# Moving an untaken branch ahead of the last copies, and one more drain on GpSimd

## The chip, the cores and the metric

The kernel runs on one core of one Trainium2 chip. The metric is the device time of one execution in microseconds (us); lower is better. The engines are PE (matmuls; PEld is its weight load), DVE (VectorE), ACT (ScalarE), POOL (GpSimd) and SP (SyncE, which here issues loads). Each engine has a sequencer that runs its queue in order; a "q" behind an engine's name marks an instruction that the sequencer itself runs, such as a wait, a branch or a drain.

## The reference

Windowed attention over (8, 8, 576, 64), whose output rows are then routed, one expert a token, through a mixture of eight two-layer networks:

```python
scores = np.where(mask, scale * q @ k.T, -1e9)        # 0 <= i - j < 64
attn = exp(scores - max); attn /= sum(attn) + 1e-9
x = (attn @ v) reordered to (4608, 512)
logits = xn @ en.T / tau                               # rows of x and emb, normalised
expert_idx = argmax(logits, axis=1)
out[mask_e] = gate_w[mask_e, None] * (np.maximum(x[mask_e] @ w1[e], 0) @ w2[e])
```

Here w1 is (8, 512, 1024) and w2 (8, 1024, 512), all float32. How many tokens an expert gets is known only when the kernel runs.

## The kernel before, in words

The first third computes attention tile by tile and puts each finished row of x into a table in DRAM, sorted by expert, with an indirect DMA that POOL issues (`place`, L444, 36 of them). The rest works through the table in groups. A group is one expert's rows: kind F is two slots of 128 rows, kind H one slot. 21 groups (`GS`, numbered 0 to 20; 39 slots) always run; how many rows each expert has decides which expert a group serves. Up to six further groups follow, each inside a branch (`tail`, L997, nested): they run only if the tokens need more groups than the fixed ones. With the inputs timed here the branch is passed over.

`step(g)` (L938) overlaps three groups: it splits group g's second-layer weights into two parts (`renew`, ACT casts L151 and DVE subtracts L154), has SP load the next group's (`load2`, L837), finishes the slots of group g-1, runs the first layer of group g+1 (L861, or L898 for kind H) and then the second layer of group g (L920). `finish(a)` (L925) is ACT's copy of a slot's result out of PSUM, scaled by the gate (L929), into one of four `o` buffers, and then POOL's indirect DMA that scatters the 128 rows to `out` (L930). The order in each engine's queue is the order in which these calls are written.

Group 20 is of kind H. Step 19 finishes the two slots of group 18, step 20 the two of group 19, and after the loop the one slot of group 20 is finished. Then every engine loads the number of groups (`values_load`, L1200) into a register, compares it (L997), jumps over the further groups, and runs a few semaphore instructions in their place. The kernel's closing lines (drains, a handshake of all engines, clearing of semaphores) have the line of the launch, L1220; its opening ones L1212. PSUM has four banks in the ring `ph` (first layer) and four in the ring `po` (second layer).

Of the kernel before, what the change touches and what calls it, by code (L numbers as in the profile page):

```python
# [46 lines left out]
GS = len(ALWAYS)  # L47
NH = ALWAYS.count("H")
KIND = ALWAYS + "F" * ((N + EARLY * P) // 256 + E - 1 - GS)
SLOT = []  # L50
# [35 lines left out]
def attention_moe(ctx, tc, q, k, v, emb, tau, w1, w2, kc, kt, out):  # L86
    nc = tc.nc
# [12 lines left out]
    def weave(*chains):  # L100

        chains = list(chains)
        while chains:
            chains = [c for c in chains if next(c, chains) is not chains]


    rings, turn = {}, {}
# [9 lines left out]
    def take(name):  # L117
        key, tiles = rings[name]
        turn[key] += 1
        return tiles[(turn[key] - 1) % len(tiles)]  # L120
# [598 lines left out]
    xb, xt, xp, ph, hp, po = {}, {}, {}, {}, {}, {}  # L719
# [8 lines left out]
    def load_x(a):  # L728

        src, b = rows(a), take("xb")  # L730
        xb[a] = b
        for q in range(4):
            note(a, nc.sync.dma_start(b[32 * q:32 * q + 32].rearrange("i (t f) -> i t f", t=4),
                                      src[:, q * P:(q + 1) * P].rearrange("(t i) f -> i t f", i=32)))

    def load_rest(*slots):

        for a in slots:
            note(a, nc.sync.dma_start(rest[:, a], rows(a)[:, DM:ROW]))
# [25 lines left out]
    def x_parts(a):  # L765
        x_turned(a)
        x_hi(a)
        x_lo(a)
# [9 lines left out]
    def gate_root(k):  # L778
        a0, a1 = BATCH[k]
        t, m, t0, t1 = gk[k] = [take("gin")[:, :a1 - a0]] + [take("gsm")[:, :a1 - a0] for _ in range(3)]  # L780
        gk[k] += [rest[:, a0:a1, :E], rest[:, a0:a1, C_SS - DM]]
        nc.gpsimd.tensor_tensor(out=t1, in0=gk[k][5], in1=half.to_broadcast([P, a1 - a0]), op=ALU.pow)

    def gate_logits(k):

        t, m, t0, t1, L, ss = gk[k]
        sh = list(t.shape)
        nc.vector.reduce_max(out=m, in_=L, axis=AX.X)
        yield
        nc.vector.tensor_scalar(out=t0, in0=t1, scalar1=1e-30, scalar2=None, op0=ALU.max)  # L790
        yield
        nc.vector.tensor_tensor(out=t, in0=L, in1=m.unsqueeze(2).to_broadcast(sh), op=ALU.subtract)
        yield
        nc.vector.reciprocal(t1, t0)
        yield
        nc.vector.tensor_tensor(out=t1, in0=ss, in1=t1, op=ALU.mult)
        yield
        nc.vector.tensor_tensor(out=t0, in0=t0, in1=t1, op=ALU.add)
        yield
        nc.vector.tensor_scalar(out=t0, in0=t0, scalar1=0.5, scalar2=1e-6, op0=ALU.mult, op1=ALU.add)  # L800
        yield
        nc.vector.reciprocal(t1, t0)
        yield
        nc.vector.tensor_tensor(out=t, in0=t, in1=t1.unsqueeze(2).to_broadcast(sh), op=ALU.mult)
        yield

    def gate_exp(k):
        t = gk[k][0]
        nc.scalar.activation(t, t, AF.Exp)

    def gate_out(k):
        t, m = gk.pop(k)[:2]
        a0, a1 = BATCH[k]
        if k:
            nc.vector.copy_predicated(rest[:, a0:a1, C_TOK - DM].bitcast(I32), again[:, a0:a1].bitcast(U32),
                                      ct[:, NT:].to_broadcast([P, a1 - a0]))
            yield
        nc.vector.reduce_sum(out=m, in_=t, axis=AX.X)
        yield
        nc.vector.tensor_scalar(out=m, in0=m, scalar1=1e-9, scalar2=None, op0=ALU.add)  # L820
        yield
        nc.vector.reciprocal(gate[:, slice(*BATCH[k])], m)
        yield
# [5 lines left out]
    def load1(g):  # L829
        e = expert(g)  # L830
        for c in range(4):
            nc.sync.dma_start(out=w1raw[c], in_=w1v[ds(e, 1), :, c].rearrange("o p f -> (o p) f"))

    def load2(g):
        e = expert(g)
        for c in range(4):
            nc.sync.dma_start(out=w2raw[c], in_=w2v[ds(e, 1), :, c].rearrange("o p k f -> (o p) k f"))  # L837

    def renew(raw, hi, lo):
        for c in range(4):  # L840
            split_hi(c, raw, hi)
        for c in range(4):
            split_lo(c, raw, hi, lo, nc.vector)
# [4 lines left out]
    def parts(g):  # L848

        return 512 // rows_of(g)  # L850
# [32 lines left out]
    def layer1_part(g, part):  # L883
        if KIND[g] == "H":
            return layer1_half(g, part)
        for f in range(parts(g) * part, parts(g) * (part + 1)):
            layer1(g, f)
        hidden(g, part)
# [14 lines left out]
    def turn_half(g, i):  # L903

        ph[g, i] = take("ph")
        for f in range(4):
            nc.tensor.transpose(ph[g, i][:, f * P:(f + 1) * P], hr[g, i][:, f * P:(f + 1) * P], ident)
        hidden(g, i)

    def layer2(g, between=lambda: None):  # L910

        n = rows_of(g)
        hh, hl = (x[:, :8 * n].rearrange("p (f n) -> p f n", n=n) for x in hp[g])
        for a in SLOT[g]:
            po[a] = take("po")
        for f in range(8):
            for j, a in enumerate(SLOT[g]):
                at = slice(j * P, (j + 1) * P)
                for i, (xx, ww) in enumerate(((hh, w2h), (hh, w2l), (hl, w2h))):
                    nc.tensor.matmul(po[a], lhsT=xx[:, f, at], rhs=ww[f // 2][:, f % 2],  # L920
                                     start=(f == 0 and i == 0), stop=(f == 7 and i == 2))
            if f == 3:
                between()

    def finish(a):  # L925

        tok = rest[:, a, C_TOK - DM:C_TOK - DM + 1].bitcast(I32)
        o = take("o")
        nc.scalar.activation(o, po.pop(a), AF.Copy, scale=gate[:, a:a + 1])  # L929
        d = nc.gpsimd.indirect_dma_start(  # L930
            out=out, out_offset=bass.IndirectOffsetOnAxis(ap=tok, axis=0), in_=o, in_offset=None,
            bounds_check=N - 1, oob_is_err=False)
        d = getattr(d, "ins", d)
        for w in outs:
            tc.declare_no_dep(d, w, reason="a token has one expert, and its row comes out alike in every slot")
        outs.append(d)

    def step(g):  # L938

        more = g + 1 < GS  # L940
        if g >= 2:
            renew(w2raw, w2h, w2l)
            if more:
                load2(g + 1)
        for a in SLOT[g - 1]:
            finish(a)
        k = FIRST.get(g + 1) if more else None
        if g + 3 < GS:
            for a in SLOT[g + 3]:
                load_x(a)  # L950
        n = 8 // parts(g + 1) if more else 0
        for part in range(n):
            layer1_part(g + 1, part)
            if part == 0 and k is not None:
                gate_root(k)
                weave(gate_logits(k))
                gate_exp(k)
            if part == 1 and k is not None:
                weave(gate_out(k))
            for a in SLOT[g + 2] if g + 2 < GS else ():  # L960
                if part == n // 4 + POS[a][1]:
                    x_parts(a)
        if g + 2 < GS:
            renew(w1raw, w1h, w1l)
        if g + 3 < GS:
            load1(g + 3)
        later = FIRST.get(g + 3)
        if later is not None and g + 3 < GS:
            load_rest(*range(*BATCH[later]))
        half = g + 1 < GS and KIND[g + 1] == "H"  # L970
        layer2(g, lambda: [turn_half(g + 1, i) for i in range(2)] if half else None)

    def alone(g):

        for a in SLOT[g]:
            load_x(a)
        load1(g)
        load2(g)
        load_rest(*SLOT[g])
        for a in SLOT[g]:  # L980
            x_parts(a)
        renew(w1raw, w1h, w1l)
        renew(w2raw, w2h, w2l)
        k = FIRST[g]
        gate_root(k)
        weave(gate_logits(k))
        gate_exp(k)
        weave(gate_out(k))
        for part in range(8 // parts(g)):
            layer1_part(g, part)  # L990
        layer2(g)
        for a in SLOT[g]:
            finish(a)

    def tail(g, total):
        if g < len(SLOT):
            with tc.If(total > KIND[:g].count("F")):  # L997
                alone(g)
                tail(g + 1, total)
# [79 lines left out]
    more = [psm2.tile([P, 512], F32, name=f"ph{i}") for i in (2, 3)]  # L1079
# [115 lines left out]
    layer2(0, shared_rows)  # L1195
    for g in range(1, GS):
        step(g)
    for a in SLOT[GS - 1]:
        finish(a)
    total = nc.values_load(meta[:1, 3:4], min_val=0, max_val=SLOTS,  # L1200
                           skip_runtime_bounds_check_because="computed within these bounds")
    tail(GS, total)


_INS = ["q", "k", "v", "moe_expert_emb", "moe_tau", "moe_w1", "moe_w2"]
# [18 lines left out]
```

## Time and profile before

| | us |
|---|---|
| median of 3 runs | 676.1 |
| lowest and highest | 674.77, 676.26 |
| profiled execution | 673.69 |
| its span, first to last instruction | 671.9 |

One execution was profiled. Its views group instructions by source line; busy time is the engine's own, while sequencer instructions (waits, register loads, branches, drains) count as idle. A view of one line lists its instructions with their shortest, median and longest duration in ns, and the start of the first and the last in us from the span's start. The chain of waits follows the work that ended last back to what released it. Matmul starts are recorded; their ends are modelled.

### The profile page before, as it was taken

The numbers are of one execution on the slowest core, as the hardware profiler recorded it, in microseconds if no ns is written. First come the engines' busy times: TensorE is split into PE (matmuls) and PEld (weight loads), VectorE is DVE, ScalarE is ACT, GpSimd is POOL, SyncE is SP. The second block draws the span as 40 slices with busy tenths as digits, with TensorE's granted clock in tenths as the row PEclk, the third lists the DMA queues.
The fourth block names the chain that finished last, engine by engine and source line by source line (L and its number), as shares of the span: only waits on it lengthen the run. The fifth ranks groups of instructions, "written<-read, shape, count | busy, mean of one in ns | idle before, by whom it ended". The sixth has DMA issues, their size and how long they took to land.

```text
span 671.9 us, 19511 instructions
## 1 busy us (share of the span) xinstructions
PE 637.5 (95%) x7564; PEld 568.1 (85%) x7564; DVE 462.5 (69%) x978; ACT 392.7 (58%) x591; POOL 204.5 (30%) x243
## 2 busy tenths in 40 slices
PE   7899999989989799999999999999999999999991
PEld 7788888878879789988998898998889998999880
DVE  2588898889977875567646877557665776656630
ACT  4587787778743345456645765636575466545640
POOL 0223555455564413221222321222022331131111
PEclk9999999999969899999999999999999999999996
DMA  8999989887552459884688688775796976757311
GB/s 222 239 242 265 261 224 231 224 237 170 147 190 98 145 147 316 288 282 153 222 267 271 226 265 292 220 263 188 250 308 208 286 270 224 226 201 281 97 63 34
DMA packets 122021, 146.86 MB, mean 219 GB/s; under 512 B 52406, under 2 KB 85046, under 8 KB 121921
## 3 DMA queue, kind: packets, MB, share of 16 engines
q1 hardware_dynamic: 115024, 125.19, 62.9%
q0 software_dynamic: 6000, 19.18, 7.6%
q8 instruction: 61, 1.00, 0.7%
q10 hardware_dynamic: 896, 1.18, 0.6%
q14 instruction: 40, 0.32, 0.2%
HBM read 123.09 MB, written 23.20 MB: 218 GB/s over the span
## 4 chain that ended last, share of the span: by engine, by line
PE 73%; DVE 10%; DMA 5%; issue 5%; ACT 2%; SPq 2%; POOL 1%; POOLq 0%; DVEq 0%; ACTq 0%
PE ph L861 30%; PE po L920 30%; PE score L254 2%; PE ph L898 2%; PE turned L192 2%; PE pair L306 2%; DMA raw<-in_q 1%; DVE aP L295 1%; DVE xr L326 1%; PE back L343 1%; PE misc L360 1%; PE pair L311 1%; DMA v<-in_v 1%; DVE aO L291 1%; DVE sm L266 1%
## 5 line engine op out<-in xcount | busy, mean ns | idle before, releaser
L861 PE MATMUL ph<-xh,w1h 128*128 128x256 f32 x576 | 163.7, 284 | 2.0 <-ACT xh L759 2.0
L861 PE MATMUL ph<-xl,w1h 128*128 128x256 f32 x576 | 163.0, 283 | 1.2 <-POOL xl L763 1.2
L861 PE MATMUL ph<-xh,w1l 128*128 128x256 f32 x576 | 163.0, 283 | 0.0
L920 PE MATMUL po<-w2h,hl 128*128 128x512 f32 x312 | 122.9, 394 | 0.0
L920 PE MATMUL po<-w2h,hh 128*128 128x512 f32 x312 | 122.4, 392 | 0.0
L920 PE MATMUL po<-w2l,hh 128*128 128x512 f32 x312 | 122.3, 392 | 0.0
L875 DVE SCALAR_TENSOR_TENSOR hl<-ph,hh 128x512 fp32r<-128x512 f32 x78 | 53.3, 689 | 96.2 <-ACT hh L871 96.2
L930 POOL DMA_INDIRECT out<-o,rest x39 | 48.1, 1233 | 222.8 <-ACT o L929 217.3
L154 DVE TENSOR_TENSOR w2l<-w2raw,w2h 128x1024 fp32r<-128x1024 f32 x80 | 94.7, 1219 | 27.6 <-ACT w2h L151 25.8
L861 PEld LDWEIGHTS ph<-xh,w1h 128*128 128x128 f32 x576 | 110.2, 191 | 3.0 <-ACT xh L759 2.1
L861 PEld LDWEIGHTS ph<-xl,w1h 128*128 128x128 f32 x576 | 110.1, 191 | 2.2 <-POOL xl L763 1.4
L861 PEld LDWEIGHTS ph<-xh,w1l 128*128 128x128 f32 x576 | 110.1, 191 | 0.0
L151 ACT CAST w2h<-w2raw 128x1024 fp32r<-128x1024 f32 x80 | 81.9, 1050 | 44.1 <-PE po L920 36.9
L154 DVE TENSOR_TENSOR w1l<-w1raw,w1h 128x1024 fp32r<-128x1024 f32 x80 | 94.1, 1234 | 10.9 <-ACT w1h L151 10.6
L763 POOL TENSOR_TENSOR xl<-xt,xh 128x512 fp32r<-128x512 f32 x39 | 50.4, 1294 | 108.2 <-ACT xh L759 108.2
L871 ACT ACTIVATE hh<-ph 128x512 fp32r<-128x512 f32 x78 | 46.1, 595 | 57.4 <-PE ph L861 50.1
L151 ACT CAST w1h<-w1raw 128x1024 fp32r<-128x1024 f32 x80 | 78.0, 1046 | 0.0
L920 PEld LDWEIGHTS po<-w2h,hl 128*128 128x128 f32 x312 | 58.6, 188 | 13.0
L920 PEld LDWEIGHTS po<-w2l,hh 128*128 128x128 f32 x312 | 58.6, 188 | 12.6
L920 PEld LDWEIGHTS po<-w2h,hh 128*128 128x128 f32 x312 | 58.6, 188 | 12.4
L759 ACT CAST xh<-xt 128x512 fp32r<-128x512 f32 x39 | 24.2, 620 | 59.3 <-DVE xt L748 58.1
L274 POOL TENSOR_TENSOR sm<-sm,st 128x512 f32<-128x512 f32 x36 | 37.4, 1040 | 63.2 <-DVE st L270 16.7
(175 smaller groups left out, 1003.9 us busy)
## 6 DMA issues: line engine op xcount, KB each, us to landing
w1raw<-in_moe_w SPq DMA_DIRECT2D x80, 512.0 KB, 4.0
w2raw<-in_moe_w SPq DMA_DIRECT2D x80, 512.0 KB, 6.2
xb<-xs SPq DMA_DIRECT2D x156, 64.0 KB, 4.6
raw<-in_q SPq DMA_DIRECT2D x64, 144.0 KB, 4.4
v<-in_v SPq DMA_DIRECT2D x64, 144.0 KB, 5.1
raw<-in_k SPq DMA_DIRECT2D x56, 144.0 KB, 4.5
xs<-xr SPq DMA_DIRECT2D x12, 264.0 KB, 4.3
rest<-xs SPq DMA_DIRECT2D x39, 8.0 KB, 3.1
```

What stands on the lines that cost most here:

```text
L151: nc.scalar.copy(hi[c], raw[c])
L154: eng.tensor_tensor(out=lo[c], in0=raw[c], in1=hi[c].bitcast(F32), op=ALU.subtract)
L192: nc.tensor.transpose(to[:, j // 3, j % 3 * I:(j % 3 + 1) * I], rl[n][:, j, 2 * i:2 * i + 2].rearrange("p h d -> p (h d)"), ident[:I, :I])
L254: nc.tensor.matmul(score[64 * z:64 * z + 64, hp, (u + 1) * P - w:(u + 1) * P], lhsT=qT[b % 2][pr, u, at:at + WIN], rhs=kT[b % 2][pr, u, at ...
L274: nc.gpsimd.tensor_tensor(out=t, in0=t, in1=st.pop(T).unsqueeze(2).to_broadcast([P, 8, WIN]), op=ALU.subtract)
L759: nc.scalar.copy(xh, t)
L763: nc.gpsimd.tensor_tensor(out=xl, in0=t, in1=xh.bitcast(F32), op=ALU.subtract)
L861: nc.tensor.matmul(o, lhsT=ww[c][:, f * P:(f + 1) * P], rhs=xx[:, c, :n], start=(c == 0 and i == 0), stop=(c == 3 and i == 2))
L871: nc.scalar.activation(hh, ph[g, part], AF.Relu)
L875: nc.vector.scalar_tensor_tensor(out=hl, in0=ph.pop((g, part)), scalar=0.0, in1=hh.bitcast(F32), op0=ALU.max, op1=ALU.subtract)
L920: nc.tensor.matmul(po[a], lhsT=xx[:, f, at], rhs=ww[f // 2][:, f % 2], start=(f == 0 and i == 0), stop=(f == 7 and i == 2))
L930: d = nc.gpsimd.indirect_dma_start(out=out, out_offset=bass.IndirectOffsetOnAxis(ap=tok, axis=0), in_=o, in_offset=None, bounds_check=N - ...
```

## The change

Step 20 no longer finishes group 19. The register load, the branch and the further groups' block now stand directly behind the loop, and the finishes of groups 19 and 20 (three slots) behind them. For the further groups the four `ph` banks are shared out, two as `ph` and two as `po`, since the banks of groups 19 and 20 still hold results there. In step 19 (`GS - 2`) POOL gets an explicit drain, ahead of the scatters of group 18.

```diff
@@ -942,8 +942,11 @@
             renew(w2raw, w2h, w2l)
             if more:
                 load2(g + 1)
-        for a in SLOT[g - 1]:
-            finish(a)
+        if g == GS - 2:
+            nc.gpsimd.drain()
+        if more:
+            for a in SLOT[g - 1]:
+                finish(a)
         k = FIRST.get(g + 1) if more else None
@@ -1195,11 +1198,16 @@
     for g in range(1, GS):
         step(g)
-    for a in SLOT[GS - 1]:
-        finish(a)
+
     total = nc.values_load(meta[:1, 3:4], min_val=0, max_val=SLOTS,
                            skip_runtime_bounds_check_because="computed within these bounds")
+    banks = rings["ph"][1]
+    ring(banks[:2], "ph")
+    ring(banks[2:], "po")
     tail(GS, total)
+    for g in (GS - 2, GS - 1):
+        for a in SLOT[g]:
+            finish(a)
```

## Rows read from the trace of the kernel before

**Rows 1.** The page: busy time of the engines, share of the span, instructions.
```profile
PE 637.5 (95%) x7564; PEld 568.1 (85%) x7564; DVE 462.5 (69%) x978; ACT 392.7 (58%) x591; POOL 204.5 (30%) x243
```

**Rows 2.** The chain of waits from 630 us on: start, duration, what.
```profile
634.27 2.81 PE ph L898 x12
...
658.73 0.72 POOL out L930
```

**Rows 3.** The timeline's end, PE and ACT: start, duration, instruction [idle before it <- releaser].
```profile
657.04 0.39 PE L920 MATMUL po<-w2h,hl 128*128 128x512 f32 x1
...
652.00 1.05 ACT L151 CAST w2h<-w2raw 128x1024 fp32r<-128x1024 f32 x1 [1.74 <-PE po L920]
652.96 1.26 ACT L929 ACTIVATE o<-po,gate 128x512 f32<-128x512 f32 x2
657.51 0.69 ACT L929 ACTIVATE o<-po,gate 128x512 f32<-128x512 f32 x1 [3.29 <-issue]
```

**Rows 4.** The timeline of POOL from 600 us to the end.
```profile
620.57 1.29 POOL L763 TENSOR_TENSOR xl<-xt,xh 128x512 fp32r<-128x512 f32 x1 [4.12 <-ACT xh L759]
636.27 1.26 POOL L930 DMA_INDIRECT out<-o,rest  x1 [14.41 <-ACT o L929]
637.83 0.97 POOL L930 DMA_INDIRECT out<-o,rest  x1 [0.30 <-ACT hr L901]
653.92 1.25 POOL L930 DMA_INDIRECT out<-o,rest  x1 [15.12 <-ACT o L929]
...
658.47 0.97 POOL L930 DMA_INDIRECT out<-o,rest  x1 [2.03 <-ACT o L929]
```

**Rows 5.** The branch's line on POOL: count, ns min/median/max, first and last start.
```profile
L997 POOLq EVENT_SEMAPHORE  x5: 17/43/3547, 659.2 to 663.1; - x5
...
L997 POOLq INC_SWDGE_SEM  x1: 1679/1679/1679, 663.2 to 663.2; - x1
```

**Rows 6.** The closing line, POOL in two stretches and SP in one: columns as in rows 5.
```profile
L1220 POOLq DRAIN  x1: 6192/6192/6192, 664.9 to 664.9; - x1
...
L1220 POOLq EVENT_SEMAPHORE  x3: 17/17/17, 671.2 to 671.8; - x3
...
L1220 SPq EVENT_SEMAPHORE  x12: 27/28/28, 664.8 to 665.5; - x12
```

**Rows 7.** The opening line on POOL.
```profile
L1212 POOLq INC_SWDGE_SEM  x1: 31/31/31, 0.1 to 0.1; - x1
...
L1212 POOLq DRAIN  x1: 169/169/169, 0.3 to 0.3; - x1
```

**Rows 8.** The two lines that issue indirect DMAs, over the whole span.
```profile
L444 POOL DMA_INDIRECT xs<-xr,pi x36: 973/1004/1776, 65.3 to 228.3; - x36
...
L930 POOL DMA_INDIRECT out<-o,rest x39: 967/1039/2567, 252.5 to 658.5; - x39
```

**Rows 9.** The scatter's line from 636 us on: time from issue to landing.
```profile
DMA to landing us min/median/max: 5.6/5.6/5.6
```

**Rows 10.** The branch's line on PE, DVE and ACT.
```profile
L997 PEldq COMPARE_BRANCH  x1: 4192/4192/4192, 655.0 to 655.0; - x1
...
L997 DVEq COMPARE_BRANCH  x1: 72/72/72, 653.7 to 653.7; - x1
L997 DVEq EVENT_SEMAPHORE  x1: 21/21/21, 656.9 to 656.9; - x1
...
L997 ACTq COMPARE_BRANCH  x1: 45/45/45, 658.1 to 658.1; - x1
L997 ACTq EVENT_SEMAPHORE  x1: 17/17/17, 658.5 to 658.5; - x1
```

**Rows 11.** The register load ahead of the branch, on ACT.
```profile
L1200 ACTq TENSOR_LOAD <-meta x1: 461/461/461, 657.5 to 657.5; - x1
```

**Rows 12.** The page: DMA issues of the second-layer weights, KB each, us to landing.
```profile
w2raw<-in_moe_w SPq DMA_DIRECT2D x80, 512.0 KB, 6.2
```

## The prediction

> **What bounds the kernel now.** I read the page first: PE is busy for 95% of the span [rows 1], so almost everything before the last matmul is priced by PE, and an edit that leaves PE's work alone can only act after it. Then the chain of waits, from its end: it walks back along PE until 634.27 us and ends with the last scatter of GpSimd (POOL) at 658.73 + 0.72 = 659.45 us [rows 2]. The span is 671.9 us. So 12.5 us lie behind the last piece of the chain, because that view ends at the last instruction that is not a sequencer's. This change is about those 12.5 us, and they are found by asking for the lines that only sequencers run.
>
> In order of time: the last matmul starts at 657.04 and lasts 0.39 [rows 3]; ACT copies it at 657.51 for 0.69 [rows 3]; POOL issues its scatter at 658.47 for 0.97 [rows 4]. Then the line of the branch on POOL: five semaphore waits from 659.2 to 663.1, one of them 3.547 us long, which is the landing of that scatter, and an INC_SWDGE_SEM of 1.679 us [rows 5]. Then the kernel's end on POOL: one DRAIN of 6.192 us starting at 664.9, and from 671.2 to 671.8 the last handshakes [rows 6]. SP's 12 semaphore instructions of that line run from 664.8 to 665.5 beside the drain, 0.06 us apart, and hold nobody up there [rows 6]. The sum: 663.1 (landed) + 0.1 + 1.68 + 6.19 + 0.83 = 671.9. No matmul, copy or transfer runs in the last 8.8 us.
>
> **What the 6.19 us are.** The same two instructions stand at the program's start, where no scatter had been issued: the DRAIN took 0.169, the INC_SWDGE_SEM 0.031 [rows 7]. At the end 36 + 39 = 75 scatters have gone through POOL's queue [rows 8] and no DRAIN of POOL stands between. So I read both as prices per scatter issued since the last drain: 6.192 / 75 = 0.083 us each for the DRAIN, (1.679 - 0.031) / 75 = 0.022 for the other. That is an inference from two points each; its rivals are below.
>
> **The change, part by part.**
>
> *The explicit drain* stands on POOL's queue in step 19, behind the subtraction at 620.57 that ends at 621.86 and before the scatter at 636.27; POOL sits idle for 14.41 us there, waiting for ACT [rows 4]. 75 - 5 = 70 scatters have been issued by then, so my estimate is 70 x 0.083 = 5.8 us, done by about 628. Behind it waits only that scatter, 8 us later. Cost on the path: zero. If the cover were gone, the scatters of two slots would land later; the first reader of that is the o buffer of the last copy, and the scatter of 637.83 lands 5.6 us after its issue [rows 9], at 643.4, against a copy at 657.51 [rows 3]: 14 us more cover. Upper bound for the explicit drain on the path: still zero, unless it holds other engines (last rival).
>
> *The branch ahead of the copies.* On POOL, the register load, the compare and the waits for landings now come behind the scatter of 637.83. They wait for its landing at 643.4, then INC_SWDGE_SEM takes at most 1.68 us: done by 645.3 at the latest. The next scatter waits for ACT until 653.92 [rows 4]: 8.6 us of cover. This takes 1.68 us and its gaps (about 0.1) out of the end. Even a slow jump fits: PE's compare took 4.192 us and DVE went on 3.1 us behind its own [rows 10].
>
> On ACT, load, compare and jump come behind the cast at 652.00 and before the copies at 652.96 [rows 3]. The load took 0.461 us [rows 11] and the jump reached the next instruction 0.45 us after the compare began [rows 10], all of it sequencer work that can run while the cast lasts (until 653.05). So the first two copies begin 0.1 to 0.3 us later. POOL is idle for 2.03 us before the last scatter [rows 4], so about 1.8 us of such a delay cost nothing; the third copy waits for PE anyway. Cost: zero, bound above by the fetch rival.
>
> PE, DVE and SP have no copy or scatter behind the branch, and their branches stay at the same place; PE's slow compare ends at 659.2 [rows 10], before the landing. Zero.
>
> *The end.* Last matmul, copy, scatter and landing stay: 663.1. POOL goes from its last scatter straight to the closing DRAIN, with 5 scatters (0.41 us at 0.083) and a landing in front of it. Drain price there: between 0.17 [rows 7] and 6.19 [rows 6]; I take 0.4, since the row that it should resemble is the one with few scatters before it. What is late next: SP's list of waits, hidden now, becomes the last: its 12 instructions at 0.06 us, the wait for the last scatter taken to stand among the first, give 0.65 us after the landing, and POOL's 0.4 lies beside it. So the new end is 663.1 + 0.65 + 0.83 = 664.6 instead of 671.9.
>
> *The ring lines* only hand the untaken branch other PSUM banks; nothing of it runs. Zero.
>
> **Sum.** -1.78 (INC_SWDGE_SEM and gaps) - 6.19 (drain) + 0.65 (SP's list) = -7.3 us. The profiled execution took 673.69 us, 1.8 us more than its span, so it would take 666.4. The median of the runs is 676.1, 2.4 us above the profiled one; the difference lies in work that the change doesn't touch, so I forecast 676.1 - 7.3 = **668.8 us**.
>
> One bound below: the wait for the last landing took 3.547 us [rows 5], and nothing here shows what sets its length; half of it, 1.8 us, taken away would give 667.0. Above: copies 0.5 us later than I think, 669.3; with the scatter of the runs about their median (+-0.7) the forecast's own range is 667 to 670.
>
> **A rule against it.** The traces show jumps of two kinds: PE and DVE lost 4.2 and 3.1 us, ACT 0.45 [rows 10]. The Trainium skill (Runtime: NRT & Kernel Launch, section Instruction fetch mechanics) says that a taken branch whose target is not in the present two-page window has to fetch its page before execution goes on. PE's and DVE's numbers agree with it; ACT's would then be a target inside the window. By it ACT's branch, moved up by a few instructions with the target still behind a block of about the same length, could fall on the other side of a page. This is the next rival.
>
> **Rivals.**
> 1. *ACT's jump is slow.* Compare at about 652.6, next instruction 3.1 to 4.2 us later, 655.7 to 656.8, instead of 653.1. Copies at 0.58 us pitch, first scatter 0.95 us after a copy begins, scatters 1.56 apart [rows 4]: last scatter at 656.7 + 3.1 = 659.8 up to 660.9, instead of 658.47. It costs 1.3 to 2.4 us: 670.1 to 671.2. Against: ACT's branch moves by only a handful of instructions. 9%.
> 2. *The drain's price is per drain, not per scatter.* Then the explicit one changes nothing and the closing one takes 6.19 again. If it runs beside the landing: 659.45 + 6.19 + 0.83 = 666.5, gain 5.4, 670.7 us (5%). If only after it: 663.1 + 6.19 + 0.83 = 670.1, gain 1.8, 674.3 us (3%). For it: there is only one long drain to look at. Against: 0.169 at the start, and the two short ones that follow in the same line.
> 3. *The copies wait for the branch on PE as well.* If what stands behind the branch waits for every engine's skipped block to be accounted for, the copies start only after PE's 659.2 [rows 10]: three copies, scatters at 660.2, 661.7, 663.3, so the last is 4.8 us late; gain 2.5, 673.6 us. Against: before, ACT and POOL passed their branch without waiting for PE. 4%.
> 4. *The explicit drain fences all engines* (the side that makes it slower). PE would stop at 634.27 [rows 2] until the weights issued at 636.7 have landed (row median 6.2 us [rows 12], about 642.9) and the drain (5.8 us) is over: 648.7, a stall of 14.4 us. It decides from 7.3 us on; the whole price gives 676.1 - 7.3 + 14.4 = 683.2. Against: it names no operand, and the register loads of the branch, which name one, ran on each engine at its own time. 4%.
>
> **How the numbers follow.** The forecast has 72%; rivals 1 to 4 have 9, 8, 4 and 4%; 3% for what I didn't think of, such as another placement of code that costs or gives back a few us. The range takes in the forecast with its bounds, rival 1 and the cheap half of rival 2: 666.8 to 671.6. What a measurement can tell here is about 0.2%, 1.35 us: faster 0.94 (all but rival 4 and a part of the unknown), same 0.01, slower 0.05.
>
> **What would show it.** In the profile after: POOL's branch line near 638 to 645, with an INC_SWDGE_SEM of under 0.2 us (2 scatters x 0.022); a DRAIN of step 19 of 5 to 6.5 us starting near 622; the closing DRAIN ending within 0.5 us of the last landing; last scatter at 658.5; span 664 to 665. Wrong if: the closing DRAIN still takes 6 us (rival 2); ACT's first copy starts after 655.5 (rival 1) or only after PE's compare ended (rival 3); PE has a hole behind 634 (rival 4).

## The result, and the profile after

The changed kernel took 670.44 us in the median of 5 runs (668.62 to 672.12), the kernel before 676.1 (674.7 to 678.74): a ratio of 0.9893, 95% interval 0.9867 to 0.992. The forecast was 668.8 us; 0.9893 x 676.1 is 668.9. The two medians alone give 0.9916, inside the interval. Two more sets of the changed kernel, timed later beside the kernel before, gave 0.9918 (0.9894 to 0.9942) and 0.9889 (0.9857 to 0.992). The three ratios stand for 7.2, 5.5 and 7.5 us.

The profiled execution of after is its slowest, 672.12 us with a span of 670.3. The page's first lines:

```profile
span 670.3 us, 19515 instructions
...
PE 638.2 (95%) x7564; PEld 568.6 (85%) x7564; DVE 463.0 (69%) x978; ACT 393.6 (59%) x591; POOL 205.6 (31%) x243
```

PE's share is that of [rows 1]. The spans alone hide what happened: the last copy starts at 657.51 us before [rows 3] and at 664.40 after, 6.9 us later, although both run the same instructions up to step 19. Of this, 6.6 us were already there at 232 us (time of before), behind the attention part, and they stay until the last matmul (657.04 before [rows 3], 663.63 after); the other 0.3 us lie between that matmul and the copy and come up again below. PE's end lay between 655.6 and 664.6 us over the thirteen profiles of this study. So the end has to be measured from a point inside it. I call the time from the start of the last copy to the end of the span the *tail*: 14.4 us before, 5.9 after. For the second set of the changed kernel I had expected a tail of 5.5 to 6.5 us and a time 6 to 8.5 us lower; its median is 6.6 us lower (5.5 by the ratio), but its profile has a tail of 6.73. That miss goes with the landing of the last scatter, 0.84 us later than in the profile after (table at the end of the experiments).

The timelines of PE (its last matmul), ACT and POOL, for [rows 3, 4] (start, duration, instruction, [idle before it <- releaser]):

```profile
663.63 0.39 PE L920 MATMUL po<-w2h,hl 128*128 128x512 f32 x1
```
```profile
658.59 1.05 ACT L151 CAST w2h<-w2raw 128x1024 fp32r<-128x1024 f32 x1 [1.75 <-PE po L920]
659.85 1.27 ACT L929 ACTIVATE o<-po,gate 128x512 f32<-128x512 f32 x2 [0.20 <-ACTq L1000]
664.40 0.69 ACT L929 ACTIVATE o<-po,gate 128x512 f32<-128x512 f32 x1 [3.29 <-issue]
```
```profile
627.16 1.29 POOL L763 TENSOR_TENSOR xl<-xt,xh 128x512 fp32r<-128x512 f32 x1 [4.11 <-ACT xh L759]
642.86 1.26 POOL L930 DMA_INDIRECT out<-o,rest  x1 [14.41 <-ACT o L929]
644.43 0.97 POOL L930 DMA_INDIRECT out<-o,rest  x1 [0.30 <-POOLq L1000]
660.81 0.97 POOL L930 DMA_INDIRECT out<-o,rest  x1 [15.41 <-ACT o L929]
662.09 0.97 POOL L930 DMA_INDIRECT out<-o,rest  x1 [0.30 <-issue]
665.36 0.97 POOL L930 DMA_INDIRECT out<-o,rest  x1 [2.31 <-ACT o L929]
```

The sequencers' lines by source line (count, ns min/median/max, first and last start in us): the explicit drain (L946), the branch on POOL, ACT and PE (L1000), and the closing line (L1228), where POOL's row is of the stretch to 669.2 and SP's to 669.5. They answer to [rows 5, 6, 10].

```profile
L946 POOLq DRAIN  x1: 7142/7142/7142, 627.1 to 627.1; - x1
...
L1000 POOLq EVENT_SEMAPHORE  x5: 17/43/43, 644.3 to 649.8; - x5
...
L1000 POOLq INC_SWDGE_SEM  x1: 226/226/226, 649.9 to 649.9; - x1
...
L1000 ACTq COMPARE_BRANCH  x1: 45/45/45, 659.1 to 659.1; - x1
L1000 ACTq EVENT_SEMAPHORE  x1: 17/17/17, 659.7 to 659.7; - x1
...
L1000 PEldq COMPARE_BRANCH  x1: 3752/3752/3752, 661.6 to 661.6; - x1
...
L1228 POOLq DRAIN  x1: 3829/3829/3829, 665.1 to 665.1; - x1
...
L1228 SPq EVENT_SEMAPHORE  x12: 27/28/18572, 650.1 to 669.3; - x12
```

What to see. POOL's branch is over at 650.2, and the next scatter waits until 660.81 for ACT. The explicit drain is entered by the sequencer at 627.12, just ahead of the start of the subtraction (627.16); from that one's end, 628.45, it lasts 5.81 us, to 634.26, and 8.6 us of idle time follow. The closing drain is entered at 665.13, ahead of the last scatter's issue, which ends at 666.33; it ends at 668.96, 0.25 us after the last landing (668.71 in the trace's record of semaphores). SP's one long wait ends at the same landing, and the eleven short ones behind it bring SP to the handshake 0.73 us later.

One cost of the change lies ahead of the tail. From the start of the last matmul to that of the last copy it takes 0.47 us before and 0.77 after. It is 0.77 in all nine profiles in which the copies stand behind a branch over work for PE, and 0.47 to 0.48 in the four others (before, and of the experiments below the drain alone, no branch, no work for PE). By the trace ACT's wait for PE ends at 664.06, and the copy begins at 664.40; what holds it for that time isn't shown. So the moved branch costs 0.29 us here, which tails don't contain.

### The profile page after: what moved, and what is told of

Same layout as the page of the kernel before. It is cut to its first block, busy times and chain, and to the rows that moved or that the text cites. A ratio compares the mean times of both kernels' runs of the same rounds, so it can differ in the third digit from the quotient of the medians.

```text
span 670.3 us, 19515 instructions
## 1 busy us (share of the span) xinstructions
PE 638.2 (95%) x7564; PEld 568.6 (85%) x7564; DVE 463.0 (69%) x978; ACT 393.6 (59%) x591; POOL 205.6 (31%) x243
## 5 line engine op out<-in xcount | busy, mean ns | idle before, releaser
L920 PE MATMUL po<-w2h,hl 128*128 128x512 f32 x312 | 122.9, 394 | 0.0
L920 PE MATMUL po<-w2h,hh 128*128 128x512 f32 x312 | 122.4, 392 | 0.0
L920 PE MATMUL po<-w2l,hh 128*128 128x512 f32 x312 | 122.3, 392 | 0.0
L920 PEld LDWEIGHTS po<-w2h,hl 128*128 128x128 f32 x312 | 58.6, 188 | 13.0
L920 PEld LDWEIGHTS po<-w2l,hh 128*128 128x128 f32 x312 | 58.6, 188 | 12.7
L920 PEld LDWEIGHTS po<-w2h,hh 128*128 128x128 f32 x312 | 58.6, 188 | 12.4
```

## The experiments

Beside the timed ratio, one number of each profile is used: the time from the last landing to the end of the span. It was 8.90 us before and 1.57 after. It leaves out how long the landing itself takes, which differs from profile to profile.

**The branch moved, without the drain.**

```diff
-        if g == GS - 2:
-            nc.gpsimd.drain()
```

> The changed kernel without the explicit drain. Theory (each scatter since the last drain costs the drain 0.083 us, and the drain works on the scatters that have landed while the last one is still under way): INC_SWDGE_SEM takes about 1.6 us at 645 to 650 where nobody waits; the closing drain deals with 75 scatters, 6.2 us from the end of the last scatter's issue on; tail 1.9 + 6.2 + 0.8 = 8.9 us, gain 5.4 us against before. If the drain only starts once everything has landed: tail 5.5 + 6.2 + 0.8 = 12.5, gain 1.8. Rival (a fixed price per drain): the same as the theory here; the next one tells them apart.

Ratio 0.9942 (0.9919 to 0.9965), 3.9 us; tail 8.98 us; 4.76 us from landing to end. The branch's line (L998) and the closing line (L1226) on POOL:

```profile
L998 POOLq INC_SWDGE_SEM  x1: 1619/1619/1619, 643.5 to 643.5; - x1
...
L1226 POOLq DRAIN  x1: 7408/7408/7408, 659.1 to 659.1; - x1
```

INC_SWDGE_SEM costs what it did, but where POOL is idle. The drain ends at 666.53, 6.20 us after the last scatter's issue ended (660.33), while that scatter landed at 662.62. So the drain works through the others while the last one is under way. The tail of 8.9 us came out as worked out. The timed gain, 3.9 us, is under the 5.4 that I had taken from the two tails: those contain the landing, which in the profile before came 3.58 us after the issue's end and here 2.29. From landing to end the gain is 8.90 - 4.76 = 4.14 us, less 0.29 ahead of the copy 3.85.

**The drain, with the branch in its old place.**

```diff
+        if g == GS - 2:
+            nc.gpsimd.drain()
         for a in SLOT[g - 1]:
             finish(a)
```

> The kernel before with the explicit drain alone; branch and copies in the old order. Theory: INC_SWDGE_SEM stays on the path but with 5 scatters since the drain instead of 75 takes 0.1 to 0.2 us instead of 1.68; the closing drain 0.2 to 0.5 instead of 6.19; SP's list of waits (0.65 us) is no longer hidden. Tail 5.5 + 0.2 + 0.7 + 0.8 = 7.2, gain 7 us: nearly all of the change's gain, with the branch's move worth 0.2 to 1.3 us on top. Rival (a fixed price per drain): closing drain 6 us again, tail 12.9, gain 1.5. Rival (the move of the branch carries the gain): under 2 us as well.

Ratio 0.9905 (0.9887 to 0.9922), 6.4 us; tail 6.50 us; 2.02 us from landing to end. The branch's line (L999) and the closing one (L1222):

```profile
L999 POOLq INC_SWDGE_SEM  x1: 279/279/279, 661.5 to 661.5; - x1
...
L1222 POOLq DRAIN  x1: 462/462/462, 661.8 to 661.8; - x1
```

Both instructions that stood on the path have lost their length with 5 scatters since the last drain instead of 75: 1.679 to 0.279, 6.192 to 0.462. The drain alone gives as much as the changed kernel did in the same set (0.9918, the intervals overlap). With the drain in place the branch's move is worth 2.02 - 1.57 = 0.45 us at the end, less 0.29 ahead of the copy about 0.2 us, too little for the timed runs; without the drain it is worth the 3.85 us above. The two edits take out largely the same time. The tail of 6.50 instead of the expected 7.2 is again a shorter landing (2.54 us after the issue's end, not 3.58); from landing to end it took 2.02 us, not the 1.7 of the expectation.

**More drains.** A drain in step 10, and two, one behind the other, in step 19.

```diff
+        if g == 10:
+            nc.gpsimd.drain()
         if g == GS - 2:
             nc.gpsimd.drain()
+            nc.gpsimd.drain()
```

> The changed kernel with a drain more in step 10 (53 scatters issued by then) and two directly one behind the other in step 19 (17 since the drain of step 10). Theory (0.083 us for each scatter since the last drain, counted behind the work that is still running ahead of it): about 4.4 us in step 10, 1.4 in step 19, and 0.1 to 0.2 for its second one; closing drain as in the changed kernel, under 0.5 us behind the last landing. Rival (a fixed price per drain after scatters): about 5.8 to 6 us in step 10 and again in step 19, and the second one of step 19 either 6 or 0.1.

The three drains' lines, and ahead of the first two the subtraction that still ran (timeline of POOL):

```profile
429.90 1.31 POOL L763 TENSOR_TENSOR xl<-xt,xh 128x512 fp32r<-128x512 f32 x1 [1.54 <-ACT xh L759]
...
L946 POOLq DRAIN  x1: 5763/5763/5763, 429.9 to 429.9; - x1
```
```profile
618.97 1.29 POOL L763 TENSOR_TENSOR xl<-xt,xh 128x512 fp32r<-128x512 f32 x1 [4.12 <-ACT xh L759]
...
L948 POOLq DRAIN  x1: 2801/2801/2801, 618.9 to 618.9; - x1
...
L949 POOLq DRAIN  x1: 53/53/53, 621.8 to 621.8; - x1
```

Counted from the subtractions' ends (431.21 and 620.26) the drains took 4.42 us for 53 scatters and 1.47 for 17, that is 0.083 and 0.086 each; the last took 0.053 for none. With 5.81 for 70 in the changed kernel this is one straight line. A fixed price per drain is out. So is a price for POOL's other work or for the time gone by: POOL's engine ran 201 instructions in the 430 us ahead of the first of these drains and 35 in the 183 us between it and the second, so that it would be 0.022 and 0.042 us an instruction, or 0.010 and 0.008 a microsecond. Every scatter here moves 128 rows, so a price per scatter can't be told from one per row. This kernel was executed once, with the profiler; it has no ratio.

**No branch at all.**

```diff
-    total = nc.values_load(meta[:1, 3:4], ...)
-    banks = rings["ph"][1]
-    ring(banks[:2], "ph")
-    ring(banks[2:], "po")
-    tail(GS, total)
```

> The changed kernel without register load, branch and further groups' block (left out; these inputs need none of them). Theory: the branch's own work is hidden in the changed kernel, so its tail stays within 0.3 us, except for one thing: in the profiles 15 of a last scatter's 16 landings came at 1.7 us after its issue ended and the last at 3.6 (before) and 2.4 (after), while instruction code was being fetched by PE behind its jump. If that fetch is what holds up the last landing, the tail is 0.6 to 1.8 us shorter here: 4.1 to 5.3 us. If not, 5.7 to 6.1.

Ratio 0.9895 (0.9872 to 0.9918); tail 5.18 us; 1.51 us from landing to end, against 1.57: the branch's own handling is hidden in the changed kernel. But all 16 landings of the last scatter (the trace has 16 semaphore updates for each, one for each part of it) were there 1.73 us after its issue ended, where the changed kernel's profile had 2.38 and the kernel before 3.58.

**A block without work for PE.** In `alone`, the two layers and the finishes are left out.

```diff
-        for part in range(8 // parts(g)):
-            layer1_part(g, part)
-        layer2(g)
-        for a in SLOT[g]:
-            finish(a)
```

> The changed kernel with the further groups' two layers and finishes left out (these inputs don't need them): the block then has nothing for PE, so PE neither compares nor jumps, while SP, DVE and ACT still do. Theory (the code that PE fetches behind its jump holds up one of the 16 landings of the last scatter): all 16 landings within 1.7 to 1.8 us of the issue's end, as without any branch (1.73), instead of 2.4 and 3.2 in two runs of the changed kernel; tail 5.2 us. Rival (any engine's fetch does it, or the handling of the skipped block): the last landing at 2.3 us or later, tail 5.8 or more.

Ratio 0.9889 (0.9869 to 0.991); tail 5.16 us; last landing at 1.72 us. One detail was not as I wrote: PE still compares, in 0.223 us instead of some 4. SP, ACT and DVE jump as ever. PE's branch line (L995), then the DMA view of the stretch from the last scatter to its landing, first of the changed kernel and then of this one (queue, kind: packets, MB, share of 16 engines):

```profile
L995 PEldq COMPARE_BRANCH  x1: 223/223/223, 654.2 to 654.2; - x1
```
```profile
q0 software_dynamic: 80, 0.22, 17.1%
q8 instruction: 1, 0.02, 2.3%
```
```profile
q0 software_dynamic: 80, 0.22, 21.0%
...
out<-o,rest POOLq DMA_INDIRECT x1, 2.7
```

The scatter's 80 packets are the same; beside them the changed kernel moves one packet of instruction code, and that packet is gone with PE's long jump. This edit takes work of ACT and POOL out of the block too; the kernel with 12 matmuls below shifts PE's jump alone.

**The last copy shared by ACT and DVE.**

```diff
-    def finish(a):
+    def finish(a, both=False):
...
-        nc.scalar.activation(o, po.pop(a), AF.Copy, scale=gate[:, a:a + 1])
+        t, n = po.pop(a), 256 if both else DM
+        nc.scalar.activation(o[:, :n], t[:, :n], AF.Copy, scale=gate[:, a:a + 1])
+        if both:
+            nc.vector.tensor_scalar(out=o[:, n:], in0=t[:, n:], scalar1=gate[:, a:a + 1], scalar2=None, op0=ALU.mult)
...
-            finish(a)
+            finish(a, g == GS - 1)
```

> The changed kernel with the last slot's copy shared: ACT scales columns 0 to 255, DVE 256 to 511. DVE is through its jump 0.8 us before PE ends (663.18 against 664.02 in the profile after). Theory: the copy (0.69 us) shrinks to 0.40 to 0.50 us, the scatter starts 0.2 to 0.3 us sooner, all else stays: 0.2 to 0.3 us less from the end of PE to the end, too little for the timed runs to tell. Rival (the two engines get in each other's way in PSUM, or DVE's jump is later than PE's end): no gain, or up to 0.5 us lost.

Ratio 0.9908 (0.989 to 0.9927). The two halves ran one behind the other; the timeline of ACT and DVE:

```profile
659.67 0.47 ACT L930 ACTIVATE o<-po,gate 128x256 f32<-128x256 f32 x1 [3.29 <-issue]
...
660.18 0.48 DVE L932 TENSOR_SCALAR o<-po,gate 128x256 f32<-128x256 f32 x1 [4.00 <-ACT o L930]
```

From the copy's start to the end of the scatter's issue it took 2.24 us instead of 1.93: 0.3 lost. DVE waited for ACT's semaphore; whether the program has to order two readers of one PSUM bank wasn't tried.

**The drain without cover**, between the scatters of group 19 and that of group 20.

```diff
-        if g == GS - 2:
-            nc.gpsimd.drain()
...
     for g in (GS - 2, GS - 1):
+        if g == GS - 1:
+            nc.gpsimd.drain()
         for a in SLOT[g]:
```

> The changed kernel with its explicit drain moved from the gap in step 19 to the place between the scatters of group 19 and that of group 20, where POOL has 2 us of idle time. Theory: 74 scatters x 0.083 = 6.1 us from the end of the second scatter's issue on; 2 us of it are hidden, the last scatter starts about 4.3 us later than it would; closing drain short; tail 5.9 + 4.3 = 10.2 us, gain against before 4.2 instead of 8.5 in these profiles. Rival (a fixed price per drain): the same place of the last scatter, but 6 us more behind it: tail 16, slower than before.

Ratio 0.9958 (0.9938 to 0.9978); tail 10.12 us, against 10.2 worked out. The drain's line and POOL's timeline around it:

```profile
L1208 POOLq DRAIN  x1: 8209/8209/8209, 657.1 to 657.1; - x1
...
658.02 0.97 POOL L930 DMA_INDIRECT out<-o,rest  x1 [0.30 <-issue]
666.18 0.97 POOL L930 DMA_INDIRECT out<-o,rest  x1 [7.19 <-issue]
```

It lasts 6.33 us from the second scatter's issue on (658.99 to 665.32), 0.086 for each of 74, and holds the third one, whose copy began at 660.33. That scatter starts 5.85 us after its copy instead of 0.96 (664.40 to 665.36 in the changed kernel), so it is 4.9 us late and not 4.3; issued when PE's jump was long over, it had landed 1.73 us after its issue ended, 0.65 sooner than in the profile after. The two misses cancel each other in the tail, so that its agreement is in part luck. The place of the drain is worth 4.2 us of tail in these two profiles, 4.9 with equal landings; the rival's 16 us is out.

**PE's branch later.** Small matmuls behind PE's last real one, ahead of the register load; 6 in one kernel, 12 in another.

```diff
+    warm(12, rings["ph"][1][0])
     total = nc.values_load(meta[:1, 3:4], ...)
```

> The changed kernel with 6 small matmuls (128x128, into a bank that nobody reads) behind PE's last real one, so that PE reaches its branch about 1.3 us later (an estimate: PE's sequencer ran 2.45 us ahead of PE's end at the compare, in matmuls of 0.23 us, and the small ones are shorter). Theory (PE's second code fetch, some 4 us behind its compare, meets the data of the last scatter and holds up one of 16 landings): that fetch now starts when the data have moved, the last landing comes 1.72 to 1.8 us after the issue's end as in the three kernels where no fetch of PE ran then (1.73, 1.72, 1.73), instead of 2.0 to 3.6 in the six others; tail 5.2 to 5.3 us instead of 5.9 to 6.7, that is 0.6 to 1.5 us less than the changed kernel. Rival (what holds it up is something else that goes with the further groups' block): landing at 2.0 us or later as before.

> The same with 12 small matmuls: PE's branch about 1.9 to 2.5 us later than in the changed kernel. Theory: the second fetch is behind the data for certain, but the first one (1.0 to 2.0 us long) may now reach into them: landing 1.72 if it ends before the data move, over 2 if not. PE's compare ends at least 1 us before the handshake, so it costs nothing by itself. Rival: no difference to the changed kernel.

> The changed kernel once more, beside the two with the later branch of PE: landing between 2.0 and 3.6 us after the issue's end, tail 5.5 to 7.1 us; time 0.5 to 1.5 us above the two others, which the timed runs will hardly tell (their intervals were 1.2 to 1.6 us to either side).

PE's compare began 2.65 us ahead of the last copy with 6 of them (2.84 in the changed kernel run beside them) and 1.22 with 12: six were too few to delay the sequencer, so my estimate of how far it runs ahead was wrong, and that kernel stayed a second look at the changed one. It landed at 3.48 us, tail 6.99, not the 5.2 to 5.3 of the expectation. With 12 the landing was at 1.73 and the tail 5.23 us; the changed kernel beside them had 1.93 and 5.43, both just under the ranges that I had given for it. The ratios are 0.9892 (0.9862 to 0.9922), 0.9865 (0.9837 to 0.9893) and 0.9889 (0.9857 to 0.992). The kernel with 12 has the shortest tail of those that leave nothing out, and the lowest ratio, but its interval overlaps with that of the changed kernel.

**The landing, over all profiles.** The last of the 16 landings of the last scatter, and the code packet of queue q8 that ran nearest to it, both in us from the end of the scatter's issue, as the trace's records of DMAs and semaphores have them:

| kernel | code packet | last landing | landing minus packet's end |
|---|---|---|---|
| before | 0.88 to 2.14 | 3.58 | 1.44 |
| after | -0.30 to 0.94 | 2.38 | 1.44 |
| after, second profile | 0.50 to 1.82 | 3.22 | 1.40 |
| after, third profile | -0.54 to 0.43 | 1.93 | 1.49 |
| branch alone | -0.19 to 0.85 | 2.29 | 1.44 |
| drain alone | -0.09 to 1.16 | 2.54 | 1.39 |
| more drains | 0.38 to 2.10 | 3.54 | 1.43 |
| shared copy | -0.87 to 0.60 | 2.03 | 1.44 |
| 6 matmuls | 1.08 to 2.04 | 3.48 | 1.44 |
| 12 matmuls | 1.54 to 2.88 | 1.73 | |
| late drain | long over | 1.73 | |
| no branch; no work for PE | none | 1.73; 1.72 | |

In nine profiles, of seven kernels, the landing follows the packet's end by 1.4 to 1.5 us, whatever else differs. In the four others it is at 1.72 to 1.73; there the scatter's 80 data packets run from 0.58 to 1.39 us, and q8's code packets were over by -0.6 us, or came only when the data had moved (12 matmuls, 1.54), or weren't there. Fifteen of the sixteen landings were there within 1.70 to 1.94 us in all thirteen. The 1.94 is that of the drain alone, and what sets it isn't shown: an 8 KB code packet of another queue (q14) runs there from 0.43 to 0.82, but before has one from 0.44 to 0.89 and its fifteenth landing at 1.73.

The trace's records of packets show what is late: five of the 80, four of 4 KB and one of 4 bytes, one behind the other. In the kernel before they run from 2.12 us, where the code packet ends (2.14), to 3.12, while all others are through at 1.38; in all nine profiles they begin between 0.02 us before and 0.39 us after the code packet's end. So one packet of code, which goes with a long jump of PE, holds up one of the scatter's sixteen parts as a whole. That the packet and that part share a DMA engine fits, but the records don't name the engine; this stays open.

## Why the prediction was right, point by point

- *Where the time lay.* Right: 8.9 us behind the last landing with nothing but sequencers at work, from [rows 5, 6]. 7.3 us of it are gone (8.90 to 1.57), the size of the forecast's sum.
- *The price per scatter.* Right for the drain: 0.083 to 0.086 us at 17, 53, 70, 74 and 75 scatters, and 0.46 us in all at 5 (the drain alone). For the changed kernel I had taken 0.4 behind the landing; it was 0.25. It was an inference from two points; the run with three drains made it a line.
- *The explicit drain hidden.* Right: 5.81 us against 5.8. The late drain shows what the cover was worth. One reading was off without harm: the 5.6 us of [rows 9] is not that of the scatter of 637.83, since the last landing of that stretch stands at 642.56 in the trace of before, not at 643.4, so the cover was 0.8 us more than I took.
- *INC_SWDGE_SEM.* The slope was right, (1.619 - 0.226) / 70 = 0.020 us a scatter. The base was wrong: I took the opening one's 0.031 [rows 7], but in the branch it is about 0.19, so 0.226 instead of under 0.2.
- *The sum.* Its size was right, its attribution was not. I booked 1.78 us to the branch's move and 6.19 to the drain, as if each edit were needed for its term. The drain alone also takes INC_SWDGE_SEM from 1.68 to 0.28, which my own price of 0.022 a scatter would have said. The move then adds 0.45 us at the end and takes 0.29 away ahead of the copy. Had I worked out each edit alone, the overlap would have shown.
- *ACT's copies.* The first two came 0.3 us later against the cast ahead of them, as forecast (0.1 to 0.3). That the third waits for PE anyway, at no cost, was wrong: it started 0.29 us later against the last matmul, on the path, a term that I had put at zero.
- *What is late next.* Right: SP's list, 0.73 us against 0.65.
- *The landing "stays".* Wrong: 3.58 us was the longest of 1.73 to 3.58. I had noticed that nothing showed what sets its length and put half of it into the low bound; the cause was PE's slow branch, which I had costed at zero because it ended before the landing. It ends in time, but its code fetch delays the landing itself.
- *ACT's jump* (rival 1) took 0.55 us, far from the 3.1 of the rival. The rule of the Trainium skill (Runtime: NRT & Kernel Launch, section Instruction fetch mechanics) fits PE's 3.5 to 4.5 us against 0.223 with an almost empty block: same instruction, nearer target. What cost more here than the jump itself is that its fetch holds up another transfer.
- *Rivals 2 to 4.* A price per drain is excluded by the run with three drains. Copies began at 659.85, before PE's compare (entered at 661.6) was through. PE ran on through step 19: its L898 matmuls start 0.22 us behind the last one of L920, and all its matmuls of that stretch keep their 6.6 us behind the kernel before.
- *The time.* 670.44 lies 1.6 us above the forecast, inside the range of 666.8 to 671.6; by the ratio it is 0.1 above. That it comes so near is in part luck: the sum left out the 0.29 us ahead of the copy, it took the landing from a single profile, which has the longest of the thirteen, and the other two sets of timed runs gave 5.5 and 7.5 us for the 7.3 forecast. What I called measurable, 0.2%, was too fine: the intervals came out at 0.17 to 0.32% to either side, while the attention part moves by several us from run to run (its last indirect DMA was issued by 226.3 to 235.0 us in the thirteen profiles).

## What to carry to other kernels

Look behind the last instruction that a view counts as work: drains, semaphore bookkeeping and handshakes can be a per cent of a kernel. Where an instruction's length grows with what was issued since the last one of its kind, as POOL's drain does here, one more of them in an idle gap can pay for itself; and cost two edits that touch the same stretch each alone before adding their gains.

## What the runs showed of the hardware that I had not expected

- A DRAIN of POOL costs 0.083 to 0.086 us for every indirect DMA issued since the drain before, although in the kernel before all of them had landed when it began: 6.19 us for 75. INC_SWDGE_SEM takes 0.020 us for each, on top of about 0.19. All these DMAs move 128 rows.
- A DRAIN of POOL is entered before the engine is through with the instruction ahead of it, so its recorded length includes that: 7.14 us, of which 5.81 are its own.
- One 16 KB packet of code (2.3% of 16 engines' time in a stretch of 3.4 us) delays one of a scatter's 16 landings until 1.4 to 1.5 us after its own end, by up to 1.9 us (3.58 against 1.73).
- ACT's last copy starts 0.29 us later where it stands behind a branch over work for PE (0.77 us from the last matmul's start against 0.47); what holds it is not known.
